# Gate and value stage in three groups of 768 tokens instead of four batches of 576

## The chip, the cores and the metric

The kernel runs on one core of one Trainium2 chip. The metric is device time in microseconds (us). Three runs of the kernel before took 777.82 to 782.80 us, with a median of 781.1 us.

## The reference

The input is attention over 4 batches, 8 heads, 576 tokens and a head width of 64, so 2304 tokens of 512 values. Three parts follow each other, all in float32 (the weights `w_gate`, `w_val` and `w_out` come as float64):

```
x = attention with 128 positive random features (exp of projections)      # 2304 x 512
e = argmax(normalised x @ normalised expert_emb.T / tau); g = its probability
x = g * (relu(x @ w1[e]) @ w2[e])                                         # 8 experts, 512 -> 1024 -> 512
out = (silu(x @ w_gate) * (x @ w_val)) @ w_out                            # 512 -> 1536 -> 512
```

The change lies in the last line, between the expert output and the product with `w_out`.

## The kernel before, in words

**Stages.** The first stage does the attention and the routing, token tile by token tile. The second stage applies the experts, one batch of 576 tokens after the other: it computes all tokens of a batch with the batch's commonest expert, and has a branch (not taken here) for the other experts. The third stage, `p3`, computes the gate and the value products and `silu(gate) * value`, and stores it to a DRAM buffer `hds`. The fourth, `p4`, reads it back and multiplies by `w_out`. The inner matmuls split every float32 operand into a high and a low part of the type `float32r` (`hi_lo`, line 90: a ScalarE cast for the high part, a VectorE subtraction for the low part) and add three products (`HALVES`, line 22).

**The experts.** For each batch `expert` (line 902) runs four units `mm1` and then four units `mm2`; each unit is fed by 1024-column weights that `fetch` loads and `hi_lo` splits. `gated` (line 889) multiplies the accumulator by the gate row on VectorE into `t` (one buffer) and adds `t` to the batch's own output tile `y_f[bt]` on GpSimd. Hooks (`todo`, line 1000) hang other work on fixed units: `split0`, `split1`, `split2` after the last `mm1` of batches 1, 2 and 3, `weights_ahead` for the first two blocks of the next stage, and `seven(0)`.

**Seven products.** The third stage treats gate and value together as a 2 by 2 block product, with seven block products in place of eight (Strassen's scheme in Winograd's form). One factor is made of the weights of a block `f` of 128 output columns (twelve blocks, `NF`): `weights_ahead` and `convert` (line 746) turn the float64 words into float32 with one ScalarE and six VectorE operations, and `seven` (line 802) forms sums and splits them. `seven` for an even block writes one pair of places, for an odd block another. The other factor is made of the tokens, once per batch: `split_y` (line 916) cuts the batch's output into a first and a second half of 288 tokens and an upper and a lower half of the 512 values; it makes seven high and low parts with `hi_lo` and four subtractions in place (line 926). Its results go over memory that is no longer used: the experts' input `arena`, the hidden values `h_all` and earlier `y_f` tiles.

**The loop.** `for f in range(NF): for bt in range(0, B, 2)` (line 1096) takes the items (block, batch) two at a time and goes through the seven products in turn, one product of the first item, one of the second. A product (line 1086) is six matmuls of 128 x 128 weights against 288 columns. The order `PRODUCTS` (line 1019) uses three accumulator tiles: `a` four times, `c` once, `b` twice. There are four buffers of `a` and two each of `b` and `c`, eight in all. Between two uses of an accumulator ScalarE copies it to `s1`, `u2` or `p5`, or VectorE adds it (`after`, line 1072). `last_product` multiplies the gate half on VectorE and the value half on GpSimd and stores both with one DMA on SP's queue. After the first pair of block `f` comes `seven(f + 1)`, after the second `weights_ahead(f + 2)`; in the second half of the blocks `out_ahead` also converts pairs of output weights, and after block 11's first pair `out_weights(0)` splits the first two of them.

**Order.** Apart from the attention stage, the order on each engine comes from a planner that simulates the program's time; it starts from the order in which the code emits instructions and may move a later one ahead where its operands are free. Instructions with `keep_in_program_order` (the first ScalarE and VectorE operation of each conversion, and `split_y`'s first cast) keep their place. Each engine then works through its own list in order.

Of the kernel before, what the change touches and what calls it, by code (L numbers as in the profile page):

```python
# [28 lines left out]
def attention_moe_ffn_kernel(  # L29
# [85 lines left out]

    HB = S // 2
    XB = NC * 2 * S
# [605 lines left out]
    ypool = ctx.enter_context(tc.tile_pool(name="ypool", bufs=B, reuse_waits="tile"))  # L723
    y_f = [ypool.tile([128, NC * S], F32, tag="y", name="y_f") for _ in range(B)]
    y_f = [y.rearrange("p (c n) -> p c n", c=NC) for y in y_f]
    LAST = B - 1
    parts_at = [[] for _ in range(B)]

    def over_x(b, run):
        return arena[:, b * XB + run * S:b * XB + (run + 1) * S]  # L730

    def over_h(run):
        return h_all[:, run * S:(run + 1) * S]

    def over_y():
        return ypool.tile([128, NC * S], F32R, tag="y", name="over_y")

    def runs_of(t):
        return [t[:, r * S:(r + 1) * S] for r in range(t.shape[1] // S)]

    def factor(bt, q, a):
        return parts_at[bt][2 * q + a].rearrange("p (c n) -> p c n", c=2)

    wf, w32 = {}, {}
# [47 lines left out]
    def parts_of(f):  # L792
        n = 7 * 2 * 128
        if f % 2:
            return [t[:, 0:n] for t in late["odd"]]
        if f == 0:
            low = wpool.tile([128, 2, NC * FU], F32R, tag="wp", name="wl")
            high = late["w"].tile([128, n], F32R, tag="wh", name="wh")
            late["even"] = [high, low.rearrange("p a n -> p (a n)")]
        return [t[:, 0:n] for t in late["even"]]  # L800

    def seven(f):

        w, parts = w32.pop(f), parts_of(f)
        wf[f] = parts
        half = DM // 2
        a11, a12, a21, a22 = (w[:, m, j * half:(j + 1) * half] for m in range(2) for j in range(2))

        def put(q, src):
            n = src.shape[-1]  # L810
            hi_lo(*(p[:, q * half:q * half + n] for p in parts), src)
# [12 lines left out]

    with ExitStack() as p2:
# [63 lines left out]
        def gated(x, ps, d, add):  # L889
            gv = x.gate.rearrange("p (j n) -> p j n", j=2)  # L890
            yv = y_f[x.bt][:, d].rearrange("p (j n) -> p j n", j=2)
            if add:
                t = tp.tile([128, S], F32, tag="t", name="t")
                t = t.rearrange("p (j n) -> p j n", j=2)
                nc.vector.tensor_tensor(out=t, in0=ps, in1=gv, op=ALU.mult)  # L895
                nc.gpsimd.tensor_tensor(out=yv, in0=yv, in1=t, op=ALU.add)  # L896
# [19 lines left out]
        def split_y(bt):  # L916

            y = y_f[bt]
            b11, b12 = y[:, 0:2, 0:HB], y[:, 0:2, HB:S]
            b21, b22 = y[:, 2:4, 0:HB], y[:, 2:4, HB:S]  # L920

            def put(q, src):
                hi_lo(factor(bt, q, 0), factor(bt, q, 1), src, pinned=q == 0)
# [4 lines left out]
            put(0, b11)  # L928
            put(1, b21)
            put(2, b22)  # L930
            sub(b11, b12, b11)
# [6 lines left out]
            yield  # L938
# [3 lines left out]
        totals, ends = [], []  # L942
# [23 lines left out]
        def no_y():  # L966
            for bt, d in [(0, NC - 1)] + [(b, d) for b in range(1, B) for d in range(NC)]:
                nc.scalar.copy(y_f[bt][:, d], zero.to_broadcast([128, S]))
# [13 lines left out]
        def split(bt, runs):  # L982
            parts_at[bt] += runs
            ends.append(split_y(bt))
            next(ends[-1])

        def split0():
            split(0, [over_x(0, r) for r in range(8)] + [over_x(1, r) for r in range(6)])
            next(ends[0], None)

        def split1():
            own = [over_x(1, 6), over_x(1, 7)] + runs_of(over_y())
            split(1, own + [over_x(2, r) for r in range(8)])
            next(ends[1], None)

        def split2():
            own = runs_of(over_y()) + [over_x(3, r) for r in range(8)]
            split(2, own + [over_h(0), over_h(1)])

# [12 lines left out]
        next(ends[2], None)  # L1012
        split(3, [over_h(r) for r in range(2, 16)])
        next(ends[3], None)
        late["odd"] = [over_y() for _ in "hl"]
# [19 lines left out]
    with ExitStack() as p3:  # L1035
# [3 lines left out]
        def tokens(bt):  # L1039

            bank_of = {
                k: fps.tile([128, HB], F32, tag=k, name=k, bufs=4 if k == "a" else 2)
                for k in "abc"
            }
            s1, u2, p5, c22 = (
                sp.tile([128, HB], F32, tag=t, name=t) for t in ("s1", "u2", "p5", "c22")
            )
            cc = sp.tile([128, 2, HB], F32, tag="cc", name="cc", bufs=3)

            def add(out, ps, other):  # L1050
                nc.vector.tensor_tensor(out=out, in0=ps, in1=other, op=ALU.add)  # L1051
# [4 lines left out]
            def last_product():  # L1056
# [3 lines left out]
                    out=hds[f][:, bt * S:(bt + 1) * S], in_=cc.rearrange("p a n -> p (a n)")  # L1060
                )

            def second():
                add(cc[:, 0], bank_of["c"], s1)
                silu(cc[:, 0])

            def sixth():
                add(c22, bank_of["a"], p5)
                add(cc[:, 1], bank_of["b"], u2)
# [12 lines left out]
            for (wq, xq, k), go in zip(PRODUCTS, after):  # L1082
                n = 0
                for c in range(2):
                    for a, x in HALVES:
                        nc.tensor.matmul(  # L1086
                            bank_of[k], wf[f][a][:, (wq * 2 + c) * 128:(wq * 2 + c + 1) * 128],
                            factor(bt, xq, x)[:, c],
# [7 lines left out]
        for f in range(NF):  # L1096
            for bt in range(0, B, 2):
                pairs = [tokens(bt), tokens(bt + 1)]
                for _ in PRODUCTS:
                    for t in pairs:  # L1100
                        next(t)
                if bt == 0 and f + 1 < NF:
                    seven(f + 1)
                elif bt == 0:
                    out_weights(0)
                else:
                    weights_ahead(f + 2)
                    if f == NF // 2:
                        two = wpool.tile([128, 2, 2, DM], F32, tag="wp", name="wo32")
                    n = f - NF // 2  # L1110
                    if n in (0, 2):
                        out_ahead(n, two[:, n // 2])
# [118 lines left out]
```

## Time and profile before

| | |
|---|---|
| median of three runs | 781.1 us (777.82 to 782.80) |
| profiled execution | 782.13 us |
| its span, first to last instruction | 780.4 us |
| mean granted TensorE clock | 0.996 |
| TensorE matmul busy | 762.6 us, 98% |
| VectorE / ScalarE / GpSimd busy | 515.4 / 370.5 / 138.9 us |
| experts' stage | about 162 to 362 us |
| gate and value stage | 361.95 to 629.75 us |
| output stage | from 629.75 us |

All durations come from the profiled execution; a step that is costed by them adds to its 782.13 us. The trace calls the engines PE (TensorE matmul), PEld (TensorE weight load, which overlaps the matmuls), DVE (VectorE), ACT (ScalarE), POOL (GpSimd) and SP (the queue that issues DMAs). "L1086" is a line of the kernel. Matmuls are pipelined: the duration of one is longer than the time from one start to the next, so a stream is measured by its whole length and count. Names such as `a<-xp,wh` say which tile is written from which; the parts of a factor that were put into old memory carry that memory's name (`xp`, `h_all`, `over_y`).

### The profile page before, as it was taken

The page shows a single profiled execution, that of the slowest core. Times are in us where ns is not written, and L with a number is a line of the kernel's source. Part 1 is how long each engine was busy: PE and PEld are TensorE (multiplying, and loading weights), DVE is VectorE, ACT ScalarE, POOL GpSimd, SP SyncE. Part 2 cuts the span into 40 slices and gives each one's busy share as a digit, 9 for nine tenths or more (in the row PEclk, how much of TensorE's full clock was granted, in tenths as well). Part 3 has the DMA queues.
Part 4 walks back from the last instruction along what each step waited for, and adds up shares of the span by engine and source line. Part 5 has one row for each costly group of instructions (what it writes and reads, how often), then busy time and mean ns, then how long its engine had stood idle before and what let it go on. Part 6 is the DMA issues. An engine that isn't in the chain of part 4 may idle for free.

```text
span 780.4 us, 16006 instructions
## 1 busy us (share of the span) xinstructions
PE 762.6 (98%) x6364; PEld 714.4 (92%) x6365; DVE 515.4 (66%) x937; ACT 370.5 (47%) x856; POOL 138.9 (18%) x197
## 2 busy tenths in 40 slices
PE   9999899999999999999999999999999999999998
PEld 8778777899999999999999999999999988888886
DVE  4798899673347776785767787678897888212220
ACT  5798569672233441445444554545445643141231
POOL 3764445100002002021111111111101100000000
PEclk9999999999999999999999999999999999999999
DMA  7635743042323342510122332224324554353233
GB/s 254 229 129 171 215 147 110 29 124 85 96 87 136 97 136 83 127 51 1 61 90 111 115 116 100 97 71 165 112 103 155 165 196 142 111 206 108 81 105 111
DMA packets 35643, 94.12 MB, mean 121 GB/s; under 512 B 4432, under 2 KB 8544, under 8 KB 35560
## 3 DMA queue, kind: packets, MB, share of 16 engines
q1 hardware_dynamic: 35400, 92.99, 36.1%
q8 instruction: 52, 0.85, 0.4%
q14 instruction: 31, 0.25, 0.1%
q10 hardware_dynamic: 160, 0.02, 0.0%
HBM read 74.05 MB, written 18.95 MB: 119 GB/s over the span
## 4 chain that ended last, share of the span: by engine, by line
PE 70%; issue 2%; DVE 0%; DMA 0%; POOL 0%; ACT 0%; POOLq 0%; ACTq 0%; DVEq 0%
PE o_ps L1131 19%; PE a L1086 18%; PE b L1086 9%; PE two L864 7%; PE two L883 5%; PE third L883 5%; PE c L1086 5%; PE third L864 2%; DMA hds<-cc 0%; DVE t L895 0%; POOL y_f L896 0%; DVE xp L95 0%; POOL cc L1058 0%; ACT o L1138 0%; ACT p L1076 0%
## 5 line engine op out<-in xcount | busy, mean ns | idle before, releaser
L1131 PE MATMUL o_ps<-xp 128*128 128x512 f32 x648 | 147.1, 389 | 0.0
L1131 PEld LDWEIGHTS o_ps<-xp 128*128 128x128 f32 x648 | 121.6, 188 | 25.2
L496 ACT ACTIVATE ph<-two,bias 128x128 f32<-128x128 f32 x288 | 78.2, 389 | 31.2 <-DVE bias L487 20.0
L95 DVE TENSOR_TENSOR xp<-h,xp 128x1024 fp32r<-128x1024 f32 (+1 forms) x36 | 34.4, 957 | 80.8 <-ACT xp L92 80.3
L1058 POOL TENSOR_TENSOR cc<-c,cc 128x288 f32<-128x288 f32 x48 | 41.0, 865 | 226.3 <-issue 205.0
L864 PE MATMUL two<-xp,wp 128*128 128x288 f32 x576 | 79.9, 297 | 0.5 <-PEq L949 0.4
L864 PEld LDWEIGHTS two<-xp,wp 128*128 128x128 f32 x576 | 77.6, 189 | 0.9 <-issue 0.9
L92 ACT CAST xp<-h 128x1024 fp32r<-128x1024 f32 (+1 forms) x36 | 30.1, 836 | 89.5 <-PE o_ps L1131 71.6
L1054 ACT ACTIVATE cc<-cc 128x288 f32<-128x288 f32 x96 | 41.9, 445 | 50.8 <-DVE cc L1051 35.4
L92 ACT CAST wp<-raw 128x1024 fp32r<-128x1024 f32 x32 | 33.6, 1049 | 54.8 <-PE two L883 29.1
L1086 PE MATMUL a<-xp,over_y 128*128 128x288 f32 x360 | 59.0, 295 | 0.0
L896 POOL TENSOR_TENSOR y_f<-y_f,t 128x576 f32<-128x576 f32 x13 | 21.6, 1662 | 184.2 <-DVE t L895 153.2
L95 DVE TENSOR_TENSOR wp<-raw,wp 128x1024 fp32r<-128x1024 f32 x30 | 47.2, 1573 | 9.6 <-ACT wp L92 9.0
L883 PE MATMUL third<-h_all,wp 128*128 128x288 f32 x384 | 52.8, 296 | 0.0
L883 PE MATMUL two<-h_all,wp 128*128 128x288 f32 x384 | 52.2, 296 | 0.0
L883 PEld LDWEIGHTS third<-h_all,wp 128*128 128x128 f32 x384 | 51.7, 189 | 0.0
L1086 PEld LDWEIGHTS a<-xp,over_y 128*128 128x128 f32 x360 | 51.6, 188 | 0.0
L883 PEld LDWEIGHTS two<-h_all,wp 128*128 128x128 f32 x384 | 51.5, 189 | 0.0
L1086 PE MATMUL a<-xp,wh 128*128 128x288 f32 x240 | 49.3, 295 | 1.5 <-DVE t L895 1.5
L479 DVE TENSOR_REDUCE mx<-two 128x8 f32<-128x1024 f32 x36 | 43.9, 1220 | 9.8 <-PE two L469 9.5
L1086 PEld LDWEIGHTS a<-xp,wh 128*128 128x128 f32 x240 | 38.5, 188 | 1.7 <-DVE t L895 1.7
L1051 DVE TENSOR_TENSOR c<-a,p 128x288 f32<-128x288 f32 x48 | 21.6, 455 | 24.2 <-PE a L1086 24.1
(222 smaller groups left out, 1552.8 us busy)
## 6 DMA issues: line engine op xcount, KB each, us to landing
raw<-in_w_dram SPq DMA_DIRECT2D x68, 512.0 KB, 3.7
hds<-cc SPq DMA_DIRECT2D x48, 288.0 KB, 2.1
h<-hds SPq DMA_DIRECT2D x24, 512.0 KB, 3.5
q<-in_qx_dram SPq DMA_DIRECT2D x18, 512.0 KB, 3.8
k<-in_kx_dram SPq DMA_DIRECT2D x14, 512.0 KB, 4.3
v<-in_vx_dram SPq DMA_DIRECT2D x18, 276.0 KB, 3.9
out_dram<-o SPq DMA_DIRECT2D x18, 256.0 KB, 3.1
h<-hds SPq DMA_DIRECT2D x12, 128.0 KB, 2.0
```

The source lines that it names most:

```text
L92: go = nc.scalar.copy(hi, src)
L95: lo_eng.tensor_tensor(out=lo, in0=src, in1=hi.bitcast(F32), op=ALU.subtract)
L479: nc.vector.tensor_reduce(out=mx.rearrange("p (c a) -> p a c", a=2), in_=p.rearrange("p a (h m) -> p a h m", m=M), axis=AX.X, op=ALU.max,)
L496: nc.scalar.activation(out=ph[:, h, :], in_=p[:, h % 2, h // 2 * M:(h // 2 + 1) * M], func=AF.Exp, bias=bias[:, h:h + 1],)
L864: nc.tensor.matmul(ps[:, j], w[:, a, c, f * 128:(f + 1) * 128], xv[:, c, b, j * HB:(j + 1) * HB], start=(c == 0 and n == 0), stop=(c == NC ...
L883: late["mark"][ENG.PE] = nc.tensor.matmul(ps[:, j], w[:, a, f, :], h[:, b, j * HB:(j + 1) * HB], start=(f == 0 and n == 0), stop=(f == len ...
L896: nc.gpsimd.tensor_tensor(out=yv, in0=yv, in1=t, op=ALU.add)
L1051: nc.vector.tensor_tensor(out=out, in0=ps, in1=other, op=ALU.add)
L1054: nc.scalar.activation(out=x, in_=x, func=AF.Silu)
L1058: nc.gpsimd.tensor_tensor(out=cc[:, 1], in0=c22, in1=cc[:, 1], op=ALU.mult)
L1086: nc.tensor.matmul(bank_of[k], wf[f][a][:, (wq * 2 + c) * 128:(wq * 2 + c + 1) * 128], factor(bt, xq, x)[:, c], start=(k not in begun), st ...
L1131: nc.tensor.matmul(p, h[:, x, i * 128:(i + 1) * 128], wos[f][:, a], start=(f == 0 and k == 0), stop=(f == NF - 1 and k == 2),)
```

## The change

**Groups.** The tokens are no longer grouped by batch after the experts. `NG` = 3 groups of `GW` = 768 consecutive tokens replace four batches of 576, so a product's matmul has `GB` = 384 columns. Group 0 holds batch 0 and 192 tokens of batch 1; group 1 the other 384 of batch 1 and 384 of batch 2; group 2 the last 192 of batch 2 and batch 3. The output tiles are `y_g`; where a batch crosses a border, `gated` writes three pieces (192, 96 and 288 tokens, in either order) for one.

**Splits.** All of group 0's split hangs on the last `mm1` of batch 2, group 1's on that of batch 3. Group 2's first cut and first subtraction are made after the third `mm2` of batch 3, the rest after the experts. Places in old memory are slots of 768 columns; an odd block's weight parts lie in six such slots.

**Items.** There are 36 items (block, group), and 42 matmuls each as before. Block 0's first two groups form a pair, its third group stands alone; from then on pairs run across the blocks, (1,0)(1,1), (1,2)(2,0), (2,1)(2,2) and so on, and (11,2) is left alone at the end. ScalarE copies go straight to the place of the sum (`cc` or `c22`) and VectorE adds onto it; `s1`, `u2` and `p5` are gone, `cc` has four buffers.

**Weights.** `seven` is a generator, one cut per product. `beside(n)` says what goes with pair or lone item `n`, with `m, k = divmod(n, 3)`: for k = 1 an odd block's `seven`, then `weights_ahead` of the next even block; for k = 2 that even block's `seven`, and some output weights; for k = 0 `weights_ahead` of the next odd block. `out_ahead(4)` comes with n = 16, `out_ahead(6)` with n = 17 and `out_weights(0)` with the last lone item.

```diff
+    GB = 384
+    NG = NT // (2 * GB)
...
+    def y_pieces(bt):
+        for j in range(2):
+            t = bt * S + j * HB
+            while t < bt * S + (j + 1) * HB:
+                g, col = divmod(t, GW)
+                n = min(GW - col, bt * S + (j + 1) * HB - t)
+                at = t - bt * S - j * HB
+                yield g, col, j, at, at + n
+                t += n
...
+    QW = 2 * 128
+    def wq_at(f, q, a, n=1):
+        if f % 2 == 0:
+            ...
+            return late["even"][a][:, q * QW:(q + n) * QW]
+        row, at = {0: (0, 0), 1: (0, 1), 2: (0, 2), 3: (1, 0), 4: (1, 1), 5: (2, 0), 6: (2, 1)}[q]
+        return late["odd"][3 * a + row][:, at * QW:(at + n) * QW]
...
         put(0, w[:, 0])
+        yield
         put(2, a22)
...
+        yield
         put(3, w[:, 1])
+        yield
         put(5, w[:, 0])
...
+            pieces = list(y_pieces(x.bt))
+            if len(pieces) == 2:
+                ...
+            else:
+                for g, col, j, lo, hi in pieces:
+                    gated_piece(
+                        x, y_g[g][:, d, col:col + hi - lo], ps[:, j, lo:hi],
+                        x.gate[:, j * HB + lo:j * HB + hi], None if t is None else t[:, j, lo:hi],
+                    )
...
+            if g == 0:
+                parts_at[g] = in_x[:14]
+            elif g == 1:
+                parts_at[g] = in_x[14:] + over_y()
+            else:
+                late["odd"] = over_y()
+                parts_at[g] = [late["odd"].pop() for _ in range(2)] + in_h
...
             put(0, b11)
+            sub(b11, b12, b11)
+            yield
             put(1, b21)
             put(2, b22)
-            sub(b11, b12, b11)
...
-            (1, NU - 1): split0,
-            (2, 0): lambda: weights_ahead(0), (2, NU - 1): split1,
-            (3, 0): lambda: weights_ahead(1), (3, NU - 1): split2, (3, NU + 1): lambda: seven(0),
+            (2, 0): lambda: weights_ahead(0), (2, NU - 1): lambda: list(split_y(0)),
+            (3, 0): lambda: weights_ahead(1), (3, NU - 1): lambda: list(split_y(1)),
+            (3, NU + 1): lambda: list(seven(0)), (3, NU + 2): lambda: next(last),
...
+            c22 = sp.tile([128, GB], F32, tag="c22", name="c22")
+            cc = sp.tile([128, 2, GB], F32, tag="cc", name="cc", bufs=4)
+            def add(out, k):
+                nc.vector.tensor_tensor(out=out, in0=bank_of[k], in1=out, op=ALU.add)
...
-                lambda: nc.scalar.copy(s1, bank_of["a"]),
+                lambda: nc.scalar.copy(cc[:, 0], bank_of["a"]),
                 second,
-                lambda: nc.scalar.copy(u2, bank_of["a"]),
-                lambda: nc.scalar.copy(p5, bank_of["b"]),
+                lambda: nc.scalar.copy(cc[:, 1], bank_of["a"]),
+                lambda: nc.scalar.copy(c22, bank_of["b"]),
...
+        def beside(n):
+            m, k = divmod(n, 3)
+            f = 2 * m + k
+            yield
+            if k == 0:
+                if 0 < m < NF // 2:
+                    weights_ahead(f + 1)
+                elif m == NF // 2:
+                    out_weights(0)
+                return
+            if k == 2:
+                yield
+                yield
+                if f < NF:
+                    yield from seven(f)
+                    if f == NF // 2 + 2:
+                        late["two"] = wpool.tile([128, 2, 2, DM], F32, tag="wp", name="wo32")
+                    if f in (NF // 2 + 2, NF // 2 + 4):
+                        out_ahead(f - NF // 2 - 2, late["two"][:, (f - NF // 2 - 2) // 2])
+                else:
+                    out_ahead(6)
+                return
+            yield from seven(f)
+            yield
+            if f + 1 < NF:
+                weights_ahead(f + 1)
+            else:
+                out_ahead(4)
+        todo = [(f, g) for f in range(NF) for g in range(NG)]
+        todo = [todo[0:2], todo[2:3]] + [todo[i:i + 2] for i in range(3, len(todo), 2)]
+        for n, items in enumerate(todo):
+            both = [tokens(*at) for at in items]
+            also = beside(n)
+            for _ in PRODUCTS:
+                for t in both:
+                    next(t)
+                next(also, None)
+            for _ in also:
+                pass
```

## Rows read from the trace of the kernel before

**Rows 1.** Page, part 1: busy time and share of the span of each engine, instructions.
```profile
PE 762.6 (98%) x6364; PEld 714.4 (92%) x6365; DVE 515.4 (66%) x937; ACT 370.5 (47%) x856; POOL 138.9 (18%) x197
```

**Rows 2.** Stretches: start:end, length, busy us (count) of PE, PEld, DVE, ACT, POOL; clock, DMA.
```profile
334.90:361.90 27.00, 25.54 (x192) 25.30 (x190) 19.05 (x27) 9.40 (x14) 6.71 (x3) 1.00 0.01 2
...
361.95:629.75 267.80, 267.54 (x2017) 267.30 (x2018) 208.50 (x374) 136.85 (x311) 41.44 (x48) 1.00 0.31 111
```

**Rows 3.** Stretch of block products, line 1086 alone: PE and PEld busy (count).
```profile
361.95:629.75 267.80, 267.53 (x2016) 267.06 (x2016) 1.00 0.31 111
```

**Rows 4.** Chain that ended last, in time: start, length, what.
```profile
629.75 146.90 PE o_ps L1131 x648
```

**Rows 5.** Timeline, 83 us: start, length, engine, line, shape, count: a 384-column burst.
```profile
83.44 1.34 PEld L252 LDWEIGHTS third<-xp,en_st 128*128 128x128 f32 x8
...
83.45 1.66 PE L252 MATMUL third<-xp,en_st 128*128 128x384 f32 x8
```

**Rows 6.** VectorE groups, 361.95 to 629.75: shapes, count | busy us, mean ns | idle.
```profile
L1051 DVE TENSOR_TENSOR c<-a,p 128x288 f32<-128x288 f32 x48 | 21.6, 455 | 24.2 <-PE a L1086 24.1
...
L814 DVE TENSOR_TENSOR w<-w 128x256 f32<-128x256 f32 x44 | 22.0, 499 | 0.3
...
L95 DVE TENSOR_TENSOR over_y<-w,over_y 128x512 fp32r<-128x512 f32 x18 | 12.6, 702 | 2.2 <-ACT over_y L92 1.9
...
L95 DVE TENSOR_TENSOR h_all<-y_f,h_all 128x576 fp32r<-128x576 f32 x5 | 3.7, 756 | 1.6 <-ACT h_all L92 1.6
...
L95 DVE TENSOR_TENSOR xp<-h,xp 128x1024 fp32r<-128x1024 f32 x3 | 3.7, 1222 | 1.0 <-ACT xp L92 1.0
```

**Rows 7.** ScalarE groups, same stretch.
```profile
L1076 ACT COPY p<-b 128x288 f32<-128x288 f32 x48 | 19.0, 399 | 7.7 <-PE b L1086 7.3
...
L92 ACT CAST xp<-h 128x1024 fp32r<-128x1024 f32 x3 | 3.2, 1051 | 4.3 <-DMA h<-hds 4.3
```

**Rows 8.** Timeline, 366 us: last matmul of a product, and its copy.
```profile
365.88 0.29 PE L1086 MATMUL b<-xp,wl 128*128 128x288 f32 x1
...
366.21 0.40 ACT L1076 COPY p<-b 128x288 f32<-128x288 f32 x1 [0.30 <-PE b L1086]
```

**Rows 9.** Timeline of PE, block 10 into block 11.
```profile
607.48 0.56 PE L1086 MATMUL c<-xp,over_y 128*128 128x288 f32 x3
...
607.88 0.43 PE L1086 MATMUL a<-h_all,wh 128*128 128x288 f32 x2
```

**Rows 10.** Waits of PE, 330 to 640 us: who for whom: us in total, times, longest.
```profile
PE a L1086 <- DVE t L895: 1.5, 1, 1.5
...
PE a L1086 <- DVE c L1051: 0.3, 1, 0.3
```

**Rows 11.** Timeline, last 5 us of the stretch; in brackets idle before and releaser.
```profile
624.83 1.05 ACT L92 CAST xp<-h 128x1024 fp32r<-128x1024 f32 x1 [0.72 <-DMA h<-hds]
...
627.88 1.87 PE L1086 MATMUL a<-h_all,over_y 128*128 128x288 f32 x12 [0.26 <-DVE c L1051]
```

**Rows 12.** GpSimd groups, same stretch.
```profile
L896 POOL TENSOR_TENSOR y_f<-y_f,t 128x576 f32<-128x576 f32 x1 | 1.4, 1420 | 0.9 <-DVE t L895 0.9
```

**Rows 13.** Timeline: converting block 2's weights (first, last of six), then their last cut.
```profile
384.32 1.13 ACT L766 ACTIVATE cv_t<-raw 128x1024 f32<-128x1024 f32 x1
...
386.29 0.68 DVE L768 TENSOR_SCALAR cv_t<-cv_t 128x1024 f32<-128x1024 f32 x1
...
391.47 1.23 DVE L786 TENSOR_TENSOR w<-w,cv_t 128x1024 f32<-128x1024 f32 x1
...
400.62 0.68 DVE L95 TENSOR_TENSOR wl<-w,wh 128x512 fp32r<-128x512 f32 x1
```

**Rows 14.** Timeline: last read of block 2's raw words, next load.
```profile
390.21 1.23 DVE L782 SCALAR_TENSOR_TENSOR cv_t<-raw 128x1024 f32<-128x1024 uint32 x1
...
391.46 0.81 SPq L750 DMA_DIRECT2D raw<-in_w_dram  x2
```

More of the change, by code (lines that the diff above doesn't have):

```diff
@@ L790, in weights_ahead @@
             convert(f, (f, 0), (f, 1))
[L792 to L800, printed above, removed]
+    QW = 2 * 128
+    def wq_at(f, q, a, n=1):
+        if f % 2 == 0:
+            if "even" not in late:
+                low = wpool.tile([128, 2, NC * FU], F32R, tag="wp", name="wl")
+                high = late["w"].tile([128, 7 * QW], F32R, tag="wh", name="wh")
+                late["even"] = [high, low.rearrange("p a n -> p (a n)")]
+            return late["even"][a][:, q * QW:(q + n) * QW]
+        row, at = {0: (0, 0), 1: (0, 1), 2: (0, 2), 3: (1, 0), 4: (1, 1), 5: (2, 0), 6: (2, 1)}[q]
+        return late["odd"][3 * a + row][:, at * QW:(at + n) * QW]
     def seven(f):
-        w, parts = w32.pop(f), parts_of(f)
-        wf[f] = parts
+        w = w32.pop(f)
         half = DM // 2
@@ L809, in put @@
         def put(q, src):
-            n = src.shape[-1]
-            hi_lo(*(p[:, q * half:q * half + n] for p in parts), src)
+            hi_lo(*(wq_at(f, q, a, src.shape[-1] // QW) for a in range(2)), src)
         def both(out, x, y, op):
@@ L894, in gated, with gated_piece @@
                 t = t.rearrange("p (j n) -> p j n", j=2)
+                gv = x.gate.rearrange("p (j n) -> p j n", j=2)
                 nc.vector.tensor_tensor(out=t, in0=ps, in1=gv, op=ALU.mult)
+            pieces = list(y_pieces(x.bt))
+            if len(pieces) == 2:
+                g, col = pieces[0][:2]
+                yv = y_g[g][:, d, col:col + S].rearrange("p (j n) -> p j n", j=2)
+                gated_piece(x, yv, ps, x.gate.rearrange("p (j n) -> p j n", j=2), t)
+            else:
[4 more added lines that the diff above has]
+                    )
+        def gated_piece(x, yv, ps, gv, t):
+            if t is not None:
                 nc.gpsimd.tensor_tensor(out=yv, in0=yv, in1=t, op=ALU.add)
@@ L966, in no_y @@
         def no_y():
-            for bt, d in [(0, NC - 1)] + [(b, d) for b in range(1, B) for d in range(NC)]:
-                nc.scalar.copy(y_f[bt][:, d], zero.to_broadcast([128, S]))
+            for g in range(NG):
+                for d in range(NC):
+                    y = y_g[g][:, d, S if g == 0 and d < NC - 1 else 0:]
+                    nc.scalar.copy(y, zero.to_broadcast([128, y.shape[1]]))
         def ahead(bt):
@@ L1011, in attention_moe_ffn_kernel @@
             expert(xs[bt], bt > 0, hooks)
[L1012 to L1015, printed above, removed]
+        next(last, None)
+        late["odd"] += over_y()
     late["t"], late["n"] = wpool, 2
@@ L1037, in attention_moe_ffn_kernel, with tokens @@
         fps = p3.enter_context(tc.tile_pool(name="fps", bufs=2, space=PSUM, reuse_waits="tile"))
-        def tokens(bt):
+        def tokens(f, g):
             bank_of = {
-                k: fps.tile([128, HB], F32, tag=k, name=k, bufs=4 if k == "a" else 2)
+                k: fps.tile([128, GB], F32, tag=k, name=k, bufs=4 if k == "a" else 2)
                 for k in "abc"
             }
[L1045 to L1051, printed above, removed]
+            c22 = sp.tile([128, GB], F32, tag="c22", name="c22")
+            cc = sp.tile([128, 2, GB], F32, tag="cc", name="cc", bufs=4)
+            def add(out, k):
+                nc.vector.tensor_tensor(out=out, in0=bank_of[k], in1=out, op=ALU.add)
             def silu(x):
@@ L1094, in tokens @@
                 yield
[L1096 to L1104, printed above, removed]
-                    out_weights(0)
-                else:
[L1107 to L1112, printed above, removed]
-                    elif f + 2 >= NF:
-                        out_ahead(4 + 2 * (f + 2 - NF))
+        def beside(n):
[6 more added lines that the diff above has]
+                elif m == NF // 2:
+                    out_weights(0)
+                return
[8 more added lines that the diff above has]
+                        out_ahead(f - NF // 2 - 2, late["two"][:, (f - NF // 2 - 2) // 2])
+                else:
+                    out_ahead(6)
[17 more added lines that the diff above has]
+                pass
     with ExitStack() as p4:
```

68 lines of the change are left out of this document (25 added, 43 removed).

## The prediction

> **What bounds the kernel now.** I read the share of each engine first, then the stretches in time, then the chain of waits, and last what TensorE waited for. TensorE is busy 98% of the span and VectorE 66% [rows 1]; the granted clock is 1.00 where the change lies, the upper of its two levels (2.4 GHz), and nothing here asks it to move [rows 2]. The gate and value stage runs from 361.95 to 629.75 us. Its block products are 2016 matmuls of 288 columns, 267.53 us of 267.80 [rows 3]: one starts every 132.7 ns, and the stretch has no hole worth naming. Only two waits of TensorE stand around it: 1.5 us at its beginning, for the multiplication that frees the last bank of the experts, and 0.3 us at its end [rows 10]. So the stage lasts as long as its matmuls, and what counts is how many there are, how long each takes, and whether the other engines keep up as they do now: VectorE 208.5 us of 267.8, ScalarE 136.9, GpSimd 41.4 [rows 2].
>
> **The matmuls.** Three groups of 768 tokens need 12 x 3 x 7 x 6 = 1512 matmuls of 384 columns, for 12 x 4 x 7 x 6 = 2016 of 288. Columns times matmuls are the same; what can go is a cost per matmul. Two widths give it: 132.7 ns at 288 columns, and 146.90 / 648 = 226.7 ns at 512 in the output stage [rows 4]. The line through them is 0.4196 ns a column (2.38 columns a ns, the upper clock) and 11.9 ns fixed. At 384 columns it gives 173.0 ns; 1512 of them take 261.6 us, 5.9 us less than 267.5. One burst of eight with 384 columns stands in the attention stage and bounds this from both sides: less the length of one, its weight loads are (1.34 - 0.19) / 7 = 164 ns apart and its matmuls (1.66 - 0.33) / 7 = 190 ns [rows 5] (0.33 us is 0.29 at 288 columns [rows 8] and 96 columns more at the upper clock). That is 248 to 287 us, a gain or a loss of 19. I take 173: it comes from 2016 and 648 matmuls in streams like the new one, the burst from eight among short ones. The Trainium skill, TensorE: Matmul & The Clock Gate, section Back-to-back issue gap, gives a warm gap of columns / 2.4 + 2.5 ns; by it 504 fewer matmuls save 1.3 us and the sum below would end at 781.8. Both rows exceed that gap by ten nanoseconds, so I don't go by it.
>
> **VectorE and ScalarE in the stage.** Each item (block, group) has three additions and one multiplication on VectorE, 455 ns at 288 columns [rows 6]; with about 1.04 ns a column (0.756 at 576, 1.222 at 1024) that is 0.555 at 384. 144 of them for 192: 79.9 us for 87.4. In-place sums cost nothing, the same operands are read. Copies on ScalarE go from 0.40 to about 0.48 us [rows 7], 108 for 144. Weight work stays: per block one conversion of six operations on VectorE, from 386.29 to 392.70 with two additions between (about 0.37 from start to start), 5.7 us [rows 13], and cutting, 4 x 0.499 + 4 x 0.702 = 4.8 us at most [rows 6]. Over two blocks, three windows of 84 x 0.173 = 14.53 us, VectorE has 6 x 2.22 + 2 x 10.5 = 34.3 of 43.6 us. Averages are covered; the spread is not even.
>
> **Where it is tightest.** The blocks with even numbers are converted and cut in the one window before their use: 5.7 + 4.8 + 4.4 = 14.9 us of 14.53. But the conversion is emitted two products (2.1 us) before that window, and the last factor cut is only used at the third product, 5.2 us after it: 21.8 us for a chain that takes 17.0 now, from 384.32 to 401.30 [rows 13]. The raw words are no part of it: their next load went out 0.02 us after their last reader, far ahead of need [rows 14]. I cost this at nothing; cover gone, it is the third rival. The opening is as full: the rest of group 2's split after the experts' end (nine operations of 0.956, 8.6 us), five items' additions (11.1), both cuts (9.6), one conversion (5.7): 35.0 us in the first 36.3, with the same 5.2 us behind. Also nothing.
>
> **The two lone items.** Block 0, group 2 and block 11, group 2 run without a partner. The seven products of an item share three accumulators, and products 3, 5, 6 and 7 must wait for a copy or an addition that reads theirs. In a pair three other products (3.1 us) lie between, in a lone item one (1.04 us). Its round trip: 0.865 us to the last matmul's start, 0.33 to the copy's start [rows 8] plus 0.04 for the wider matmul, 0.48 the copy: 1.72 of 2.08, 0.36 to spare; through VectorE 0.29. Whatever stands ahead on the engine then holds TensorE. Bounds: nothing, if the queues are free or TensorE is given other products (its order already mixes blocks: block 11's product c starts before block 10's a is done [rows 9]); and one longest operation ahead of each of the four, 3 x (1.05 - 0.36) + (1.22 - 0.29) = 3.0 us [rows 6, 7], 6.0 for both. I take 0.5 for the first, which has a pair behind it to borrow from, and 1.5 for the last: there ScalarE stood for a transfer of the next stage's input, and even a pair's 3 us did not cover it [rows 11]. Behind that copy are the two additions and the last product. The last item's output weights and inputs now have to be cut in 7.27 us beside it, and the conversion of the last output weights moves ahead of the stage's end (5.7 us of VectorE, 1.1 of ScalarE, two loads on SP): part of the 1.5.
>
> **Edits with one answer.** Group 0 is split in batch 2 and group 1 in batch 3, each eleven operations of 0.956 us (10.5) for eleven, or ten, of 0.756; batch 3's second half has at most 2.9 + 1.9 us more on VectorE, 19.05 to 23.9 of 27.0 [rows 2]. If that cover failed, the last expert's weights would come late. GpSimd's gated sums of batches 1 and 2 become three pieces; three full ones of 1.42 us [rows 12] would still fit between two units of 48 x 0.133 = 6.4 us, and batch 3 has one piece as before, so the 1.5 us at the border stays. Twelve zeroing copies for 13 over the same elements, 36 stores of 384 KB for 48 of 288, the split weight slots: nothing, none is waited for.
>
> **The sum.** The profiled execution took 782.13 us (span 780.4 and 1.7 around it), 1.0 above the median of 781.1. 782.1 - 5.9 + 2.0 = 778.2; against the median 777.2.
>
> **Rivals.** First, the lone items and full windows eat the gain: one operation ahead at each round trip, 782.1 - 5.9 + 6.0 - 1.0 = 781.2, and 783.7 with half the runs' spread. For it: VectorE at 78% and in order; against: at the same load 2016 matmuls lost 0.3 us [rows 10]. Second, the edit doesn't do what it says, because a matmul's cost goes with its columns: 132.7 / 288 x 384 = 177 ns, 1512 take 267.5 as before, 783.1 with the lone items. Against it, 512 columns would take 236 and take 226.7 [rows 4]. Third, slower: the chain of an even block's weights. Where its conversion waits its turn behind the two items' additions and the conversion of output weights, it decides from 21.8 us on; at 24.7, 45% over today's 17.0, TensorE stands 2.9 us in each of five windows, 14.5 in all, and the time is 791.7. For it: 14.9 us of work in 14.5; against: the grace on both sides, and that the next window asks only 10.1. Fourth, 384 columns at the burst's 164 ns: 782.1 - 19.5 + 2.0 - 1.0 = 763.6; for it the weight loads of one burst [rows 5], against it the line through two long streams, whose fixed part it would cut to 4 ns.
>
> **How the numbers follow.** Forecast 0.55, first rival 0.20, second 0.06, third 0.12, fourth 0.05, the rest unnamed. Low end: no stall, 775.2, less half the spread of the three runs, 2.5: 772.7. High end: first and second rival, 783.7. That leaves out the third and fourth, some 0.2. A measurement of this kernel tells about 1% (773.3, 788.9) from no change. Faster by more: the fourth and a lucky edge of the forecast, 0.10; slower by more: most of the third, 0.10; the rest 0.80.
>
> **What would show it.** Right: 1512 matmuls at 173 ns, a stretch of 262 to 266 us from the same start near 362, holes in TensorE only in two windows of 7 us. Wrong: another spacing (second and fourth rival); holes in every third window, waiting for a cut of weights (third); holes before 362, if the splits crowd the last expert.

## The result, and the profile of the changed kernel

The changed kernel takes 786.92 us (median of 6 runs, 785.6 to 788.62) where the kernel before took 780.51 beside it (6 runs, 776.54 to 782.8): a ratio of 1.009, 95% interval 1.0061 to 1.012. It is 6.4 us slower; 777.2 was forecast, with a range up to 783.7. The profiled execution took 788.62 us, its span 786.6 for 780.4 before: 6.2 us to be found.

The engines' busy time, from the page, answers to [rows 1]. TensorE has 504 instructions fewer and yet 1 us more of busy time.

```profile
PE 763.6 (97%) x5860; PEld 714.3 (91%) x5861; DVE 507.9 (65%) x878; ACT 361.3 (46%) x788; POOL 154.1 (20%) x201
```

The block products alone, line 1102 now, answer to [rows 3]: start:end and length of the stretch, TensorE's and the weight loads' busy time (count), clock, DMA.

```profile
362.74:634.05 271.31, 266.77 (x1512) 265.30 (x1512) 0.99 0.31 112
```

The stage begins 0.8 us later and lasts 271.31 us for 267.80, with 4.5 us in which TensorE stands. The waits of TensorE from 300 us on (us in total, times, longest), the counterpart of [rows 10], name where:

```profile
PE a L1102 <- DVE c L1067: 4.4, 2, 4.0
PE a L1102 <- DVE t L910: 2.3, 1, 2.3
```

The border wait grew from 1.5 to 2.3 us, and the wait for an addition on VectorE from 0.3 to 4.4. There is no other. TensorE's timeline (start, length, what; in brackets the idle time before and its releaser) puts the second into the lone last item, and the chain of waits gives what came behind it; both answer to [rows 11] and [rows 4]:

```profile
622.35 1.21 PE L1102 MATMUL a<-xp,over_y 128*128 128x384 f32 x6
623.94 1.32 PE L1102 MATMUL a<-over_y 128*128 128x384 f32 x6 [0.38 <-DVE c L1067]
625.39 1.31 PE L1102 MATMUL a<-h_all,over_y 128*128 128x384 f32 x6
626.54 1.21 PE L1102 MATMUL b<-h_all,over_y 128*128 128x384 f32 x6
631.76 2.29 PE L1102 MATMUL a<-h_all,over_y 128*128 128x384 f32 x6 [4.02 <-DVE c L1067]
```
```profile
634.05 148.62 PE o_ps L1169 x648
```

Six matmuls take 6 x 0.173 = 1.04 us from start to start, so the gaps between these five groups are 0.55, 0.41, 0.11 and 4.18 us, 5.25 in all. The last group then took 2.29 us, where such a row has 1.20, and the output stage 148.62 us for 146.90. The granted clock says why; its stretches are the same columns as [rows 2] (busy time of PE, PEld, DVE, ACT, POOL, then clock and DMA):

```profile
612.00:634.05 22.05, 17.52 (x92) 16.56 (x91) 19.48 (x25) 12.24 (x22) 4.17 (x3) 0.92 0.53 179
634.05:640.00 5.95, 5.95 (x20) 4.73 (x20) 3.20 (x4) 1.14 (x2) 0.85 (x1) 0.71 0.74 235
640.00:782.00 142.00, 142.00 (x628) 117.67 (x627) 44.05 (x49) 40.08 (x56) 0.00 (x0) 1.00 0.37 121
```

After the 4 us hole the clock is at its lower level (1.2 GHz) for a while, mean 0.71 of full speed over 634 to 640 us, and back at 1.00 from 640 on. What VectorE did meanwhile is in its timeline:

```profile
625.34 1.21 DVE L95 TENSOR_TENSOR xp<-h,xp 128x1024 fp32r<-128x1024 f32 x1
626.47 1.50 DVE L782 TENSOR_SCALAR cv_t<-cv_t 128x1024 int32<-128x1024 int32 x1
627.90 1.01 DVE L1073 TENSOR_TENSOR cc<-a,cc 128x384 f32<-128x384 f32 x2
628.83 0.68 DVE L95 TENSOR_TENSOR xp<-w,xp 128x512 fp32r<-128x512 f32 x1
629.42 1.21 DVE L786 SCALAR_TENSOR_TENSOR w<-raw,cv_t 128x1024 int32<-128x1024 int32 x1
630.56 0.68 DVE L95 TENSOR_TENSOR xp<-wo,xp 128x512 fp32r<-128x512 f32 x1
631.16 0.54 DVE L1067 TENSOR_TENSOR c<-a,c 128x384 f32<-128x384 f32 x1
```

The addition of 631.16 reads accumulator a, which the fifth product had filled at about 626.7 (625.39 + 1.31); the seventh product, into the same accumulator, starts 0.06 us after its end. Between 626.47 and 631.16 not one operation stood ahead of it but six: two of the conversion of the last output weights (L782, L786: 2.7 us), the pair's last multiplications (1.0) and two cuts for the output stage (1.4). VectorE was never idle; it had the addition in the wrong place of its order.

The pace of the matmuls comes from undisturbed runs of twelve or more, in an even block (weights wh and wl) and in an odd one (weights in over_y):

```profile
508.96 0.51 PE L1102 MATMUL b<-xp,wh 128*128 128x384 f32 x2
...
511.07 1.39 PE L1102 MATMUL a<-xp,over_y 128*128 128x384 f32 x7
...
521.61 2.24 PE L1102 MATMUL a<-xp,over_y 128*128 128x384 f32 x12
523.68 2.24 PE L1102 MATMUL b<-xp,over_y 128*128 128x384 f32 x12
525.76 1.03 PE L1102 MATMUL a<-over_y 128*128 128x384 f32 x5
```

In the odd block 24 start in 525.76 - 521.61 = 4.15 us, 173 ns each, as forecast. In the even block twelve take 511.07 - 508.96 = 2.11 us, 175.8 ns. In the trace of before it was the other way round, and less: 24 of 288 columns took 3.20 us in an odd block and 3.16 in an even one, 133.3 and 131.7 ns:

```profile
443.07 0.96 PE L1086 MATMUL a<-xp,over_y 128*128 128x288 f32 x6
...
446.27 0.43 PE L1086 MATMUL a<-xp,wh 128*128 128x288 f32 x2
...
454.23 0.43 PE L1086 MATMUL a<-xp,wh 128*128 128x288 f32 x2
...
457.39 0.43 PE L1086 MATMUL a<-over_y,wh 128*128 128x288 f32 x2
```

The 6.2 us, term by term: the stage less its holes and its slow last group is 271.31 - 5.25 - 1.09 = 265.0 us, 2.5 less than the 267.5 of before; holes 5.25 for 0.3, +4.9; the lower clock 1.09 in the last group and 1.72 in the output stage, +2.8; border +0.8. That is 6.0.

### The profile page after: what moved, and what is told of

Its sections match the earlier page's. It is cut to its first block, busy times and chain, and to the rows that moved or that the text cites. A ratio compares the mean times of both kernels' runs of the same rounds, so it can differ in the third digit from the quotient of the medians.

```text
span 786.6 us, 14726 instructions
## 1 busy us (share of the span) xinstructions
PE 763.6 (97%) x5860; PEld 714.3 (91%) x5861; DVE 507.9 (65%) x878; ACT 361.3 (46%) x788; POOL 154.1 (20%) x201
## 4 chain that ended last, share of the span: by engine, by line
PE 69%; DVE 2%; DMA 1%; issue 0%; ACT 0%; POOL 0%; SPq 0%; ACTq 0%; POOLq 0%
PE o_ps L1169 19%; PE a L1102 18%; PE b L1102 9%; PE two L879 7%; PE two L898 5%; PE third L898 5%; PE c L1102 4%; PE third L879 2%; DMA h<-hds 1%; DVE xp L95 1%; ACT xp L92 0%; DVE t L910 0%; POOL y_g L925 0%; DVE cc L1073 0%; DVE cc L1067 0%
## 5 line engine op out<-in xcount | busy, mean ns | idle before, releaser
L1169 PE MATMUL o_ps<-xp 128*128 128x512 f32 x648 | 148.8, 393 | 0.0
L1074 POOL TENSOR_TENSOR cc<-c,cc 128x384 f32<-128x384 f32 x36 | 40.6, 1127 | 230.1 <-ACT cc L1070 190.5
L925 POOL TENSOR_TENSOR y_g<-y_g,t 128x192 f32<-128x192 f32 (+3 forms) x29 | 37.2, 1305 | 169.1 <-DVE t L910 169.1
L1070 ACT ACTIVATE cc<-cc 128x384 f32<-128x384 f32 x72 | 37.6, 526 | 55.3 <-DVE cc L1067 55.3
L95 DVE TENSOR_TENSOR wp<-raw,wp 128x1024 fp32r<-128x1024 f32 x30 | 39.9, 1330 | 9.8 <-ACT wp L92 9.4
L1102 PE MATMUL a<-xp,over_y 128*128 128x384 f32 x216 | 43.0, 335 | 0.0
L1102 PE MATMUL a<-xp,wh 128*128 128x384 f32 x144 | 37.0, 338 | 2.3 <-DVE t L910 2.3
L1102 PEld LDWEIGHTS a<-xp,over_y 128*128 128x128 f32 x216 | 38.3, 188 | 0.0
L886 DVE SCALAR_TENSOR_TENSOR h_all<-two,h_all 128x576 fp32r<-128x576 f32 x24 | 18.1, 756 | 24.2 <-ACT h_all L885 24.1
L885 ACT ACTIVATE h_all<-two 128x576 fp32r<-128x576 f32 x24 | 15.5, 652 | 35.2 <-PE two L879 35.2
```

The costliest lines, as they stand in the source:

```text
L95: lo_eng.tensor_tensor(out=lo, in0=src, in1=hi.bitcast(F32), op=ALU.subtract)
L886: nc.vector.scalar_tensor_tensor(out=h2[:, 1], in0=ps, scalar=0.0, in1=h2[:, 0].bitcast(F32), op0=ALU.max, op1=ALU.subtract,)
L1070: nc.scalar.activation(out=x, in_=x, func=AF.Silu)
L1074: nc.gpsimd.tensor_tensor(out=cc[:, 1], in0=c22, in1=cc[:, 1], op=ALU.mult)
L1102: nc.tensor.matmul(bank_of[k], wq_at(f, wq, a)[:, c * 128:(c + 1) * 128], factor(g, xq, x)[:, c], start=(k not in begun), stop=(n == 5), s ...
L1169: nc.tensor.matmul(p, h[:, x, i * 128:(i + 1) * 128], wos[f][:, a], start=(f == 0 and k == 0), stop=(f == NF - 1 and k == 2),)
```

## The experiments

cols288, cols512, front_wh416, front_wh288 and before_wh288 were run once each and are read by their traces; the others have 6 to 12 runs each, beside the kernel before on the same chip.

**late_out: the conversion of the last output weights, again behind the items.**

```
 beside(n), k == 2, f == NF:
-                else:
-                    out_ahead(6)
 after the loop over the items:
+        out_ahead(6)
```

> The changed kernel with one edit: the conversion of the last pair of output weights is emitted after the last item, as the kernel before does, not beside the last pair. Queue theory (the last lone item's addition waited behind three operations of that conversion on VectorE, and TensorE's clock fell in the hole): the hole of 4.0 us before the last product falls under 1 us, the granted clock stays at its upper level into the output stage, and the time falls by 5 to 8 us to 779 to 782. Round-trip theory (a lone item stalls by itself, whatever stands in the queues): a hole of 3 us or more stays and the time is 785 to 787. Stage-wide theory (the time is lost in small pieces over all windows): the hole goes, but the time falls by 4 us at most.

Measured: 782.97 us (12 runs), ratio to before 1.0013 (1.0002 to 1.0023), for 1.009 with the conversion in front. TensorE's wait at the end of the stage and the end of its chain:

```profile
PE a L1102 <- DVE c L1067: 1.7, 2, 1.0
```
```profile
628.78 146.94 PE o_ps L1168 x648
```

The hole of 4.0 fell to 1.0, and with it went the low clock: the output stage is back at 146.94 us. One moved conversion cost 6.0 us by the two ratios (0.0077 x 781; 3 to 9 by their intervals), and by the traces 2.5 us of gaps and 2.8 of the clock. Some 2.7 us of gaps stay in the lone item (0.86, 0.32, 0.17, 1.27 and 0.11); ahead of the last addition VectorE still has three cuts for the output stage and the pair's last multiplications.

**front_lone: both lone items at the front, pairs to the end.** The lone items are now block 0, group 2 and block 1, group 0; the weight work hangs on other windows, in the same order (the edits of `beside` are left out below).

```
...
-        todo = [todo[0:2], todo[2:3]] + [todo[i:i + 2] for i in range(3, len(todo), 2)]
+        todo = [todo[0:2], todo[2:3], todo[3:4]] + [todo[i:i + 2] for i in range(4, len(todo), 2)]
```

> The changed kernel with both lone items at the front: (0,0)(0,1), then (0,2) alone, (1,0) alone, then pairs (1,1)(1,2), (2,0)(2,1), (2,2)(3,0) to the last pair (11,1)(11,2); the weight work is hung on the pairs accordingly and the last pair has the end work of the kernel before. Queue theory: no hole over 0.5 us at the end, none at the front, where the planner has other products to put between, clock at its upper level; time 777 to 781. Round-trip theory: holes of 2 to 4 us move to the front, time 781 to 784. Stage-wide theory: still 784 or more.

Measured: 779.24 us (12 runs), 0.9973 (0.996 to 0.9986), faster than both kernels (by 0.3% against the one before). TensorE's only wait from 300 us on is the border's:

```profile
PE a L1102 <- DVE t L910: 2.3, 1, 2.3
```
```profile
628.04 146.94 PE o_ps L1177 x648
```

Two lone items in a row cost nothing where a pair follows, whose products TensorE takes in between. So it is not the lone item that is dear but its place: at the end nothing is left to fill with, and the output stage's cuts share VectorE. No run tells these two apart. The conversion of the last output weights runs behind the stage here as in late_out, so what front_lone adds is told by late_out beside it.

**cols288 and cols512: the same products, narrower and wider.**

```
cols288:
-                            bank_of[k], wq_at(f, wq, a)[:, c * 128:(c + 1) * 128],
-                            factor(g, xq, x)[:, c],
+                            bank_of[k][:, 0:GB if k not in begun else 288], wq_at(f, wq, a)[:, c * 128:(c + 1) * 128],
+                            factor(g, xq, x)[:, c, 0:GB if k not in begun else 288],
cols512:
+                            wide[k], wq_at(f, wq, a)[:, c * 128:(c + 1) * 128],
+                            parts_at[g][2 * xq + x][:, c * 256:c * 256 + 512],
```

> The changed kernel, in which all block-product matmuls but the first on each accumulator of an item (39 of 42) take 288 of their 384 columns; the last 96 columns of each half miss most of their sum. Only the distance between matmuls in unbroken runs is read, since VectorE's work would now bound the stage. Width theory (the part that is not columns grows with the width from 288 to 384): 131.7 to 133.3 ns as in the kernel before, 12 matmuls in 1.58 to 1.60 us. Layout theory (the new places of factors and weights cost 2 to 3 ns a matmul at any width): 135 to 136 ns, 12 in 1.62 us or more.

> The changed kernel, in which every block-product matmul takes 512 columns of its factor's place in place of 384 and writes 512; the sums are those of other columns, and 128 columns of each accumulator are read by nobody. Width theory, with 0.445 ns a column from 288 to 384: 232 ns a matmul, a stage of 351 us. Layout theory (2 to 3 ns over the output stage's 226.7): 229 ns, 347 us. Straight line of the prediction: 226.7 ns, 343 us.

Measured: 740.08 and 863.46 us. Where TensorE is not held up, twelve of 288 columns take 1.58 us in an even and in an odd block (first fence, cols288: 440.24 to 441.82 and 452.44 to 454.02), and twelve of 512 columns take 2.72 us in an odd one (second fence, cols512), 2.75 in an even one:

```profile
440.24 0.43 PE L1102 MATMUL a<-xp,wh 128*128 128x288 f32 x2
...
441.82 0.47 PE L1102 MATMUL b<-h_all,wh 128*128 128x384 f32 x2
...
452.44 0.95 PE L1102 MATMUL a<-xp,over_y 128*128 128x288 f32 x6
...
454.02 0.74 PE L1102 MATMUL c<-h_all,over_y 128*128 128x384 f32 x4
```
```profile
523.37 2.88 PE L1103 MATMUL b<-xp,over_y 128*128 128x512 f32 x12
526.09 0.39 PE L1103 MATMUL a<-xp,wl 128*128 128x512 f32 x1
```

In odd blocks the three widths give 131.7, 173 and 227 ns, a straight line within 1 ns: the rule by which I costed the matmuls holds. In even blocks they give 131.7, 175.8 and 229: 2 to 3 ns more at the two greater widths, none at 288. So it is no fixed price of the new weight slots.

**front_wh and before_wh: the even blocks' upper weight halves begun at another byte.** The tile is made 448 B longer; as it lies at the upper end of the memory, its columns then begin 32 bytes past a multiple of 512, like those of the odd blocks, and not at 480.

```
-                high = late["w"].tile([128, 7 * QW], F32R, tag="wh", name="wh")
+                high = late["w"].tile([128, 7 * QW + 112], F32R, tag="wh", name="wh")
```

> The kernel of front_lone (779.2 us), and the upper halves of the even blocks' weights begin at another byte: the tile is 448 B longer, so that its columns begin 32 bytes past a multiple of 512, as those of the odd blocks do, where before they began at 480. Theory (an even block's matmul of 384 columns costs 175.8 ns instead of 173.3 because of where these weights lie): 12 matmuls of an even block take 2.08 us instead of 2.11, 756 x 2.4 = 1.8 us less, 777.4 us. Rival (it is something else that goes with even blocks: the lower halves, the work of the other engines beside them, a cost by region of the memory): 2.11 us as before, 779.2 us.

> The kernel before with the even blocks' upper weight halves begun at the same other byte, nothing else. Theory (place of the weights): its even blocks take 1.58 us for 12 matmuls instead of 1.60, 1008 x 1.6 ns = 1.6 us less, 779 us against 780.5. Rival (something else in even blocks): 1.60 us, no difference.

Measured: front_wh 777.08 us (6 runs), 0.9943 (0.9929 to 0.9958), where front_lone had 0.9973; before_wh 782.58 us (11 runs), 1.0018 (1.0007 to 1.003). The same even block's product b in front_lone and, behind it, in front_wh:

```profile
501.82 0.51 PE L1102 MATMUL b<-xp,wh 128*128 128x384 f32 x2
...
503.92 0.51 PE L1102 MATMUL a<-over_y,wh 128*128 128x384 f32 x2
```
```profile
500.36 0.51 PE L1102 MATMUL b<-xp,wh 128*128 128x384 f32 x2
...
502.44 0.51 PE L1102 MATMUL a<-over_y,wh 128*128 128x384 f32 x2
```

2.10 us became 2.08: at 384 columns the place of the weights is what made even blocks dear. Twelve matmuls show little of it; the whole stages show more (length, then the columns of [rows 2]; the first line is front_lone's, the second front_wh288's, a further place below, the third and fourth front_wh's):

```profile
362.98:628.04 265.06, 265.06 (x1513) 265.06 (x1514) 206.55 (x324) 129.50 (x249) 37.74 (x35) 1.00 0.29 109
361.09:623.45 262.36, 262.36 (x1513) 262.36 (x1514) 206.51 (x324) 128.94 (x249) 37.76 (x35) 1.00 0.30 110
361.35:625.32 263.97, 263.97 (x1513) 263.97 (x1514) 207.04 (x324) 129.17 (x249) 37.73 (x35) 0.99 0.30 109
360.00:370.00 10.00, 8.65 (x40) 8.65 (x41) 6.51 (x9) 6.39 (x11) 1.93 (x2) 0.83 0.00 1
```

At the full clock the cheap place is worth 2.7 us; front_t and front_t_wh, further below, give the same (265.07 and 262.37). front_wh's stage shows only 1.1 of it, because its clock fell behind the wait at the border: 0.83 over ten microseconds costs 1.7. The 2.7 are more than the 1.8 expected, also because odd blocks gained. From start to start, the mean over all their matmuls fell from 174.3 to 173.3 ns from front_lone to front_wh288, though they don't read the moved weights; the long ones in front_lone stand right behind a product of an even block.

In before_wh the same shift made the even blocks dearer, against both theories that I had written down. Both took 1.60 us for twelve matmuls of the kernel before, where its even blocks already have 1.58 (3.16 for 24). Now 24 matmuls of 288 columns take 3.20 us (455.09 to 458.29):

```profile
455.09 0.42 PE L1086 MATMUL a<-xp,wh 128*128 128x288 f32 x2
...
458.29 0.43 PE L1086 MATMUL a<-over_y,wh 128*128 128x288 f32 x2
```

1008 x 1.6 ns is 1.6 us; the stage is 269.38 us long for 267.80, and the median stands 1.45 us above that of the kernel before. The place matters there too, with the other sign: the kernel before had its even blocks at the cheap place.

**front_wh416, front_wh288 and before_wh288: two more places.** As above with 16 and 48 columns more instead of 112 (416 and 288 bytes past a multiple of 512).

> The kernel of front_lone with the even blocks' upper weight halves begun 64 B earlier (416 past a multiple of 512, before 480; 32 in front_wh). Theory A (only a beginning at 32, as the moving columns have it, is cheap): 12 matmuls of an even block stay at 2.10 to 2.11 us. Theory B (480 is a bad place, most others are good): 2.08 us. The time itself is not asked: 777 to 780 us.

> The kernel of front_lone with the even blocks' upper weight halves begun 192 B earlier (288 past a multiple of 512). Theory A (only 32 is cheap): 2.10 to 2.11 us for 12 matmuls of an even block. Theory B (480 is a bad place, most others are good): 2.08 us. 777 to 780 us.

> The kernel before with the even blocks' upper weight halves begun 192 B earlier (288 past a multiple of 512; 480 took 1.58 us for 12 matmuls, 32 took 1.60). Theory A (with 288 columns, whose halves begin at 32, 160, 288 and 416 past a multiple of 512 in turn, what counts is the distance between weights and moving columns, and averages out): between 1.58 and 1.60 us. Theory B (480 alone is special, here the cheap one): 1.60 us. 780 to 783 us.

Measured, one run each: 782.19, 776.4 and 784.27 us. Twelve matmuls of an even block take 2.10 us at 416 (503.36 minus 501.26, first fence, front_wh416), twelve take 2.08 at 288 (503.52 minus 501.44, second fence, front_wh288), and with 288 columns twelve take 1.60 at 288 (456.73 minus 455.13, third fence, before_wh288).

```profile
501.26 0.52 PE L1102 MATMUL a<-xp,wh 128*128 128x384 f32 x2
...
503.36 0.51 PE L1102 MATMUL b<-xp,wh 128*128 128x384 f32 x2
```
```profile
501.44 0.51 PE L1102 MATMUL a<-xp,wh 128*128 128x384 f32 x2
...
503.52 0.51 PE L1102 MATMUL b<-xp,wh 128*128 128x384 f32 x2
```
```profile
455.13 0.42 PE L1086 MATMUL a<-xp,wh 128*128 128x288 f32 x2
...
456.73 0.43 PE L1086 MATMUL b<-xp,wh 128*128 128x288 f32 x2
```

front_wh416's stage takes 265.91 us with its clock at 0.83 from 360 to 370 us, some 264.2 without that: dear, but less so than at 480.

So 384 columns are cheap at 32 and 288 and dear at 416 and 480; 288 columns are cheap at 480 and dear at 32 and 288 in the kernel before, yet cheap at both 32 and 480 in cols288, whose moving columns begin elsewhere (always 32 past a multiple of 512, in the kernel before at four places in turn). Neither theory fits all of it: theory A fails on 288, theory B on 416. What the rule is stays open. The neighbouring tiles in that pool (weights that are not yet cut, which no block product reads) moved along with wh in each of these runs; that their place plays no part was not tried.

**front_t, and both edits: front_t_wh, after_t_wh.** In front_t the last product of the experts is multiplied into a tile of another pool, so that it needn't wait for GpSimd to have read the one tile t.

```
-                t = tp.tile([128, S], F32, tag="t", name="t")
+                if x.bt == LAST and d == NC - 1 and not x.extra:
+                    t = wpool.tile([128, NC * FU], F32, tag="raw", name="t_end")[:, 0:S]
+                else:
+                    t = tp.tile([128, S], F32, tag="t", name="t")
```

> The kernel of front_lone (779.2 us), and the last product of the last expert (d = 3) multiplied into another tile than the one that the addition on POOL still reads. Theory (the border hole of 2.3 us in the changed kernel is the wait for that one tile t, whose reader on POOL came later because the experts' last groups run in another order): the product no longer waits for POOL, the hole falls to about 0.9 us and the output stage ends 1.4 us earlier, 777.8 us. Rival (the hole is VectorE's and the banks', not the tile's): the hole stays at 2.3 us and the time at 779.2; or the split of the last group, which waits for POOL's addition of the same product, is late for its matmuls: then a new wait stands in the first 15 us of the blocks.

> Both edits at once, the candidate for the best kernel. By the two theories 779.2 - 1.4 - 1.8 = 776.0 us; by both rivals 779.2 us; with one of them 777.4 or 777.8.

> The changed kernel with only the two small edits (the last product of the experts in a tile of its own, the even blocks' upper weight halves begun 448 B earlier); the order of the items and of the conversions as in the changed kernel. Theory (the losses of the change add up: 1.4 us at the border, 1.8 us by the place of the weights, 4.4 us of holes behind the conversion of the last output weights, 2.9 us of a lower clock behind these): 786.9 - 1.4 - 1.8 = 783.7 us, with the hole of about 4 us before the last product and the output stage at 148.6 us still there. Rival (the end of the stage is late because its last item begins late): holes and clock there go too, 777 us.

Measured: front_t 778.14 us (7 runs), 0.9959 (0.9936 to 0.9982), an interval that reaches that of front_lone; the trace shows it plainly, a border wait of 0.8 us for 2.3, while the stage stays at 265.07 us:

```profile
PE a L1105 <- DVE t_end L913: 0.8, 1, 0.8
```

front_t_wh, the best of all: 776.04 us (6 runs), 0.9922 (0.9898 to 0.9946). Its stage runs from 360.81 to 623.18, 262.4 us or 173.5 ns a matmul. after_t_wh 783.33 us (12 runs), 1.0013 (1.0 to 1.0025), forecast 783.7: with these two edits alone the end is as bad as in the changed kernel, in place and size:

```profile
626.12 2.29 PE L1105 MATMUL a<-h_all,over_y 128*128 128x384 f32 x6 [3.90 <-DVE c L1070]
```
```profile
628.41 148.79 PE o_ps L1172 x648
```

The losses add up, and that the holes at the end came only of a late start is excluded.

## Why the prediction was wrong

**The last lone item: the step that failed.** I bounded it by "one longest operation ahead of each of the four", 3.0 us, took 1.5, and put the moved conversion, 5.7 us of VectorE, into that as "part of the 1.5". I had written down that the cuts fall beside this item, that the conversion moves ahead of the stage's end and that two additions and the last product wait there, and then still let one operation stand ahead of each. VectorE did them in its order: what counted is the whole sum that this order put between a product and the addition that reads it, and that was six operations and 4.7 us. Measured were 5.25 us of gaps. late_out shows the conversion to be the cause of 2.5 us of it, and of the fall of the clock, front_lone that the remainder is the item's place.

**The clock: a term that was missing.** Of the clock I wrote that "nothing here asks it to move". A hole of 4 us was outside what I had priced; behind it came 2.8 us more at the lower level. late_out, with 1.0 us as its longest hole in the stage's end, has none of this.

**The matmuls: the mechanism right, the size off.** Forecast -5.9, measured -2.5. The line through 288 and 512 columns gave 173.0 ns, and the undisturbed odd blocks, cols288 and cols512 keep to it. But I took one spacing for all blocks. The mean of 132.7 hid two prices, 131.7 and 133.3, of which the cheaper turned into the dearer one at the new width: 756 matmuls at 175.8 instead of 173.0 are 2.1 us of the missing 3.4. Without holes the stage takes 265.1 us in front_lone (362.98 to 628.04), and with the weights moved 262.4 in front_wh288 and in front_t_wh, where I had 261.6: the place of the weights is 2.7 us, the share of the odd blocks included. The 0.8 that are left are spread over the stage, and no run takes them apart. The rule that I had set aside, of the Trainium skill, TensorE: Matmul & The Clock Gate, section Back-to-back issue gap, does not fit these streams: its columns / 2.4 + 2.5 gives 162.5 ns at 384 columns, and the cheapest stream here took 173. The section gives it for an isolated matmul, which the prediction did not say.

**The border.** I let it stand that "the 1.5 us at the border stays": it became 2.3. I counted the pieces of GpSimd's work, which did not change, and not the order of the last expert's matmuls, in which the product before the last now ends later (its multiplication starts at 359.60 us, before at 358.76), with GpSimd and the last multiplication behind it on one tile:

```profile
361.93 0.76 DVE L910 TENSOR_TENSOR t<-third,gate 128x576 f32<-128x576 f32 x1 [1.57 <-POOL y_g L925]
```

front_t took 1.5 us of the wait away.

**What held.** The first lone item: no gap, for the 0.5 forecast. The third rival, the even blocks' weight chain: no wait between 362.74 and 622 us, so the cover that I had counted was enough. The first rival named the right mechanism and, for the last item, 3.0 us of the 5.25; the fourth is refuted by the odd blocks' 173 ns. The second would have fitted the even blocks alone (131.7 / 288 x 384 = 175.6 ns, measured 175.8); the odd blocks, cols512 (227 and 229 for 236) and the moved weights refute it. The time stayed within 1% of before, on the other side than I forecast.

## What to carry to other kernels

Where work is moved beside an item that has no partner to fill its gaps, sum up everything that the engine's order puts between a result and the instruction that frees its accumulator, not the longest operation in it, and put such an item where other work follows, not at the end. A hole of some microseconds in TensorE is paid twice if the clock falls behind it, as it did here behind both holes of 4 us and behind three of eight of 2.3 us, so price it with the stretch behind it. A spacing read as a mean over a stage should be read once per kind of block before it is carried to another shape.

## What was not expected of the hardware

Where weights begin in memory changes a matmul's pace by 1 to 1.4%: 173.3 against 175.8 ns at 384 columns, 131.7 against 133.3 at 288. Only the neighbours in their pool moved along. The stage changed by 2.7 us at 384 columns (front_lone to front_wh288) and by 1.6 at 288 (before to before_wh, the other way); which place is cheap depends on the shape (32 and 288 past a multiple of 512 at 384 columns, 480 in the kernel before).

After a hole of 4 us TensorE's six matmuls took 2.29 us, and the next ones ran at a mean clock of 0.71 for 6 us. The same wait of 2.3 us at the border, behind the same expert products, was followed by the lower level in three traces (front_wh, front_wh416 and cols512, 0.83 over 360 to 370 us) and not in five others (the changed kernel, late_out, front_lone, front_wh288 and cols288, 1.00). What decides between them stays open. Behind the border waits of 0.8 and 1.5 us and late_out's gaps of up to 1.27 us no fall was seen.
